# RWKV attention with a Sinkhorn-gated mixture of experts: the first three tiles and the first expert's weights in another order

## The chip, the core and the metric

The kernel runs on one core of a Trainium2 chip. The core's engines work side by side, each through its own list of instructions in order: TensorE (PE in the profile) multiplies matrices, VectorE (DVE), ScalarE (ACT) and GpSimd (POOL) work on elements, and SyncE (SP) mainly issues transfers between memory and the core. They wait for each other by semaphores. The metric is the device time of one execution in microseconds (us). Three executions of the kernel before took 1536.46, 1536.66 and 1537.26 us, so the median is 1536.66.

## What is computed

```python
def _attn_ref(r, k, v, w, u):              # r, k, v: (4, 8, 768, 48)
    state = np.zeros((B, H, D, D)); y = np.zeros_like(r)
    for t in range(S):
        kt, vt, rt = (k[:, :, t], v[:, :, t], r[:, :, t])
        cur = np.einsum('bhd,bhe->bhde', u[None] * kt, vt)
        y[:, :, t] = np.einsum('bhd,bhde->bhe', rt, state + cur)
        state = w[None, :, :, None] * state + np.einsum('bhd,bhe->bhde', kt, vt)
    return y
...
def _moe_ref(x, w_gate, w1, w2):           # N, D, E, F = 3072, 384, 8, 1024
    logits = x @ w_gate
    P = np.exp(logits - logits.max())
    for _ in range(8):
        P /= P.sum(1, keepdims=True) + 1e-09
        P /= P.sum(0, keepdims=True) + 1e-09
        P *= N / E
    for e in range(E):
        out += P[:, e:e + 1] * (np.maximum(x @ w1[e], 0.0) @ w2[e])
    return out
```

The first part is a recurrence over 768 positions for 4 batches of 8 heads with 48 channels each; w is a decay per head and channel. Its output, as a matrix x of 3072 tokens by 384, goes through a gate (eight rounds of normalizing over rows and columns, over all tokens) and through all eight experts, each with two weight matrices w1[e] (384 x 1024) and w2[e] (1024 x 384). Everything is in 32-bit floats.

## The kernel before

**Tiles.** The 3072 tokens are 24 tiles of 128; six tiles are one batch, and a state S is handed from tile to tile in a batch. Three tiles in a row (TH = 3) are a *position*, which the first expert works on together. The recurrence over 128 tokens becomes matrix products: r and k are multiplied by tables of powers of the decay, `rtab` and `ktab` (the powers come from a scan over 64 steps, and 1/w^n is the reciprocal of these powers), and a masked product of the two replaces the loop. Where a decay lies outside 0.7 to 1.1 the tables don't serve; then a flag is set and a branch (`scan_channels`, L386 to L432) works those channels step by step. With the inputs given the branch isn't taken, but each engine has to read the flag (`values_load`, L429) and branch.

**Stages of a tile**, each a function, with the names that its results have in the profile:

- `load_part`: SP loads r, k and v of a tile (`rn`, `kn`, `vn`, 192 KB each; tile 3's r and k go to a part of `hb3`).
- `prep`: POOL makes `rp` = r x `rtab`, DVE makes `kp` = k x `ktab`.
- `bonus_dot` and `bonus`: POOL makes `rk` = r x k x u, DVE sums it over channels to `dg`, and POOL makes v x `dg`.
- `stage_b`: PE transposes `rp` and `kp` (`prT`, `pkT`), ACT copies them out (`rT`, `kT`).
- `stage_c`: PE makes `pA` = kT x rT, DVE copies its upper triangle to `at` under a mask; PE makes `pu`, DVE adds it to the state (`S`).
- `stage_d`: PE makes `py` from the state and `at`; DVE adds the bonus to get `x`, and takes its maximum (`xm`) and from it a power of two as a scale (`xs`).
- `scale_x`: ACT and DVE write x as a high and a low half-precision part (`xsc`).
- `stage_e`: one DMA transposes `xsc` into `hbx` (`DMA_TRANSPOSE` on SP). The expert and the gate read `hbx`.
- `stage_f`: PE multiplies by the gate's weights (`px`), DVE writes the logits (`lparts`).

**The first expert** runs inside this loop as work for PE. `split_weights` (L151) turns its w1 and w2, loaded into `ws0`, into high and low half-precision parts in `ws1`: DVE takes maxima (`wm`, three pieces; `wma`), PE and DVE take them over the partitions (`over_partitions`, `pmax`), then ACT writes high parts and DVE low parts, three pieces of 1024 columns for each matrix. A *unit* is one call of `g1_unit` (nine matmuls `ph` of 384 columns: 128 of the 1024 hidden channels for a whole position; ACT and DVE then write `hb`, high and low) or of `g2_half` (twelve matmuls `po` for half the hidden channels of one tile). `combine_tokens` further prepares sums of tokens, on POOL above all, that the other seven experts need.

**What sets the order.** Every engine's list is written out by hand in program order (`InOrder`, L21): the order of the calls is the order on each engine. The loop at L754 runs i = 0 to 26. In iteration i it issues `prep` and the loads for later tiles, `stage_b` of tile i+1, `scale_x` and `stage_e` of tile i-2, `stage_c` of tile i, `stage_d` of tile i-1, and `stage_f` of tile i-3. So a tile's transposing DMA goes out two iterations after its `stage_c`. At two places `work` puts units into PE's list: one unit, then one or, for i over 8, two. As long as i is 4 or less, `spin(3)` takes the place of a unit: three matmuls of a zero matrix (`pz`), which compute nothing and keep PE busy. The list `side` holds the steps of splitting the weights and of `combine_tokens`; `prepare` takes one step from it, and the table STEPS says how many are taken in iteration i, ahead of and behind `stage_d`. Position 0's units come into the list when tile 2 has gone out. Whatever units are left after the loop are worked one per *tick* (L985), beside the gate's rounds; then the other experts follow, in 14 slots of long runs of matmuls.

**The opening** is all code ahead of the loop: SP's loads (L307 to L328), memsets that clear `hbx`, the flag, the branch, and behind the branch the tables. SP's loads of tile 2's and tile 3's v follow the branch too. PE spins 19 times ahead of the branch, and 5 and 4 times around the tables' transposes.

## Time and profile before

| what | value |
|---|---|
| median of three executions | 1536.66 us |
| the profiled execution, its time | 1537.3 us |
| its span, first to last instruction | 1535.4 us |
| PE busy | 1519.8 us, 99% |
| DVE, ACT, POOL busy | 1033.7, 663.5, 598.1 us (67, 43, 39%) |
| DMA moved | 143.12 MB, 93 GB/s over the span |
| chain of work that ended last | PE 94%, DVE 5% |

The profile is that of one execution. Rows of groups name line, engine, operation, and tiles as out<-in with shape, type and count; almost every row has line 29, the helper that records instructions, so the tile's name tells the place. The timeline has start and duration in us, and in brackets the idle time just ahead with what ended it. PEld is PE's weight load. "DVEq" and "SPq" are the queues of the engines, where branches and issues of DMAs are handled. The stage table gives busy time, with counts in brackets, in stretches of the span; PEclk is PE's granted clock as a share of full speed.

### The profile page before, as it was taken

The page shows a single profiled execution, that of the slowest core. Times are in us where ns is not written, and L with a number is a line of the kernel's source. Part 1 is how long each engine was busy: PE and PEld are TensorE (multiplying, and loading weights), DVE is VectorE, ACT ScalarE, POOL GpSimd, SP SyncE. Part 2 cuts the span into 40 slices and gives each one's busy share as a digit, 9 for nine tenths or more (in the row PEclk, how much of TensorE's full clock was granted, in tenths as well). Part 3 has the DMA queues.
Part 4 walks back from the last instruction along what each step waited for, and adds up shares of the span by engine and source line. Part 5 has one row for each costly group of instructions (what it writes and reads, how often), then busy time and mean ns, then how long its engine had stood idle before and what let it go on. Part 6 is the DMA issues. An engine that isn't in the chain of part 4 may idle for free.

```text
span 1535.4 us, 26169 instructions
## 1 busy us (share of the span) xinstructions
PE 1519.8 (99%) x10313; PEld 858.1 (56%) x10313; DVE 1033.7 (67%) x1714; ACT 663.5 (43%) x1168; POOL 598.1 (39%) x708
## 2 busy tenths in 40 slices
PE   8999999999999999999999999999999999999999
PEld 5677766655555555555555555555555555555555
DVE  8988877676666666667666666656666566666554
ACT  4333424434444444535454444535344444445320
POOL 8789985120213424242424324242423224242200
PEclk9999999999999999999999999999999999999999
DMA  8556623121225665675666666655445554555434
GB/s 192 104 114 113 131 49 112 51 73 55 98 58 109 88 118 86 110 107 83 116 92 125 92 117 88 126 64 98 58 62 92 61 98 56 98 60 98 55 95 129
DMA packets 186847, 143.12 MB, mean 93 GB/s; under 512 B 109537, under 2 KB 180962, under 8 KB 186722
## 3 DMA queue, kind: packets, MB, share of 16 engines
q0 software_dynamic: 44928, 61.36, 32.6%
q1 hardware_dynamic: 141584, 80.07, 19.8%
q8 instruction: 81, 1.33, 0.4%
q14 instruction: 44, 0.36, 0.1%
q10 hardware_dynamic: 210, 0.00, 0.0%
HBM read 55.39 MB, written 80.23 MB: 88 GB/s over the span
## 4 chain that ended last, share of the span: by engine, by line
PE 94%; DVE 5%; issue 0%; ACT 0%; DMA 0%; DVEq 0%; ACTq 0%
PE po L29 48%; PE bZ L29 12%; PE bY L29 12%; PE ph L29 5%; PE bA L29 5%; PE bB L29 5%; PE bC L29 2%; PE py L29 2%; PE pA L29 1%; DVE hb L29 1%; PE prT L29 1%; PE pu L29 1%; DVE at L29 0%; DVE ws L29 0%; PE pkT L29 0%
## 5 line engine op out<-in xcount | busy, mean ns | idle before, releaser
L29 PE MATMUL po<-ws,hbx 128*128 128x384 f16 x3360 | 736.8, 326 | 0.0
L29 POOL DMA_DIRECT2D accd<-stg x288 | 249.7, 869 | 694.4 <-ACT stg L29 673.8
L29 PEld LDWEIGHTS <-hbx 128*128 128x128 f16 x3504 | 334.1, 98 | 292.6
L29 PEld LDWEIGHTS <-ws 128*128 128x128 f16 x3096 | 301.8, 98 | 246.7 <-issue 3.4
L29 ACT ACTIVATE hbx<-tb 128x512 f16<-128x512 f32 x224 | 141.0, 630 | 451.6 <-DVE tb L29 451.6
L29 PE MATMUL po<-ws,hb 128*128 128x384 f16 x1248 | 323.0, 326 | 0.3 <-DVE ws L29 0.3
L29 DVE TENSOR_TENSOR tb<-bY,tb 128x512 f32<-128x512 f32 x168 | 116.1, 691 | 195.4 <-PE bY L29 195.2
L29 ACT ACTIVATE stg<-po,pe 128x384 f32<-128x384 f32 x312 | 179.1, 574 | 121.2 <-PE po L29 94.3
L29 PE MATMUL bZ<-xv,ws 128*128 128x512 f16 x840 | 227.0, 379 | 0.7 <-DVE tb L29 0.7
L29 PE MATMUL bY<-xv,ws 128*128 128x512 f16 x840 | 227.0, 379 | 0.0
L29 DVE TENSOR_TENSOR tb<-bZ,tb 128x512 f32<-128x512 f32 x168 | 115.4, 687 | 136.3 <-PE bZ L29 136.3
L29 PEld LDWEIGHTS <-hb 128*128 128x128 f16 x1248 | 121.4, 98 | 93.8 <-issue 0.8
L29 POOL TENSOR_TENSOR ucb<-rawb 128x256 f32<-128x256 f32 x84 | 75.7, 952 | 118.7 <-DMA rawb<-in_moe_w_dram 118.7
L29 DVE TENSOR_TENSOR tb<-bB,tb 128x512 f32<-128x512 f32 x112 | 77.4, 691 | 48.9 <-PE bB L29 47.0
L29 PE MATMUL ph<-hbx,ws 128*128 128x384 f16 x576 | 105.8, 329 | 1.2 <-DMA hbx<-xsc 0.7
L29 DVE SCALAR_TENSOR_TENSOR hb<-tb,hbx 128x512 f16<-128x512 f32 x112 | 77.2, 689 | 24.7 <-ACT hbx L29 19.5
L29 PE MATMUL bB<-xv,ws 128*128 128x512 f16 x336 | 90.8, 379 | 0.0
L29 PE MATMUL bA<-xv,ws 128*128 128x512 f16 x336 | 90.8, 379 | 0.0
L29 DVE SCALAR_TENSOR_TENSOR hbx<-tb,hbx 128x512 f16<-128x512 f32 x112 | 78.7, 703 | 14.7 <-ACT hbx L29 10.4
L29 ACT COPY tb<-bZ 128x512 f32<-128x512 f32 x56 | 32.8, 585 | 65.5 <-PE bZ L29 65.5
L29 ACT ACTIVATE hb<-ph 128x384 f16<-128x384 f32 x64 | 31.1, 488 | 57.6 <-PE ph L29 57.0
L29 DVE SCALAR_TENSOR_TENSOR hb<-ph,hb 128x384 f16<-128x384 f32 x64 | 35.4, 553 | 26.3 <-ACT hb L29 25.8
(166 smaller groups left out, 1539.6 us busy)
## 6 DMA issues: line engine op xcount, KB each, us to landing
accd<-stg POOLq DMA_DIRECT2D x288, 192.0 KB, 3.7
rawb<-in_moe_w_dram SPq DMA_DIRECT2D x28, 768.0 KB, 6.7
e0d<-stg SPq DMA_DIRECT2D x48, 192.0 KB, 2.1
hb<-e0d SPq DMA_DIRECT2D x48, 192.0 KB, 3.9
vn<-in_v_dram SPq DMA_DIRECT2D x24, 192.0 KB, 3.6
accd<-stg SPq DMA_DIRECT2D x24, 192.0 KB, 1.8
accd<-hb POOLq DMA_DIRECT2D x24, 192.0 KB, 4.7
rawb<-accd SPq DMA_DIRECT2D x24, 192.0 KB, 2.5
```

The source lines that it names most:

```text
L29: return lambda *a, **k: self.tc.keep_in_program_order(f(*a, **k))
```

## The change

It changes the opening and the first iterations of the loop; the stages themselves compute what they did.

- **Tables.** They stand ahead of the branch now. `wsi` holds w and 1/w; one scan of both (520 columns, twice as long) gives the powers of each, and the reciprocal is taken of four columns rather than of 260. The flag comes from the same comparison that the tables need: a maximum per partition, one transpose on PE (`pnb`) and one DVE maximum. A load of w as one row (`wrow`) is gone.
- **Loads.** Ahead of the branch stand r, k of tiles 0 and 1, v of tile 0, u, and w1 in three loads between them. All else follows the branch: v of tile 1, all of tiles 2 and 3, the gate's weights, w2, tile 4.
- **Memsets.** DVE now clears 1920 columns of `hbx` (3072 each for DVE and POOL before), POOL 3840, ACT the rest. Two of the three states are cleared inside the loop.
- **Spins.** 27 matmuls of zeros in all: 8 and 6 ahead of the branch, 4 behind it, and three in each of three places in the loop, where before there were 58 in all.
- **First three tiles.** For i below 3 (AHEAD) an iteration does `stage_d` of its own tile, then `scale_x` and `stage_e` of it (`emit`). From tile 3 on the order is the old one, so iteration 3 has no `stage_d`.
- **Weights.** w1 is split in iteration 0 (its maxima ahead of it), w2 in iterations 1 to 4. STEPS has a third number, for steps behind `emit`; in iterations 5 to 8 no step is taken.
- **First position.** When a tile has gone out, two units of a new kind, `g1_tile`, come into the list: 36 matmuls of 128 columns each (`pht`), half the hidden channels for one tile, and one ACT and one DVE operation of 512 columns behind them. There are six in place of eight `g1_unit`; six `g2_half` of position 0 follow. `work` gives two units to an iteration up to i = 14, and three from 15.

```diff
+    def g1_tile(t, j, W):
...
+        ph = ps1.tile([P, TB], F32, tag="ph", name=f"pht_{t}_{j}")
...
+        for fl in range(FHC):
+            fs = slice((j * FHC + fl) * P, (j * FHC + fl + 1) * P)
+            for c in range(KC):
+                xh_, xl_ = xall(t, 0)[:, c, :], xall(t, 1)[:, c, :]
+                T.matmul(ph[:, fl], w1h[:, c, fs], xh_, start=(c == 0), stop=False)
+                yield
+                T.matmul(ph[:, fl], w1h[:, c, fs], xl_, start=False, stop=False)
+                yield
+                T.matmul(ph[:, fl], w1l[:, c, fs], xh_, start=False, stop=(c == KC - 1))
+                yield
+        S_.activation(hh, ph, AF.Relu)
+        V.scalar_tensor_tensor(hl, ph, 0.0, hh, op0=ALU.max, op1=ALU.subtract)
...
-    for tt in range(2):
-        load_part(tt, "r", r)
-        load_part(tt, "k", k)
...
-    load_part(0, "v", v)
+    def load_w1(c):
+        Q.dma_start(raws[0][:, c], w1[0, c * P : (c + 1) * P, :])
+    load_part(0, "r", r)
+    load_part(0, "k", k)
+    load_w1(0)
     Q.dma_start(
         ub.rearrange("p h d -> p (h d)"),
...
     )
-    load_part(2, "r", r)
-    load_part(2, "k", k)
-    load_part(1, "v", v)
-    load_part(3, "r", r)
-    load_part(3, "k", k)
-    Q.dma_start(wg, w_gate.rearrange("(c p) e -> p c e", p=P))
-    for c in range(KC):
-        Q.dma_start(raws[0][:, c], w1[0, c * P : (c + 1) * P, :])
+    load_part(0, "v", v)
+    load_w1(1)
+    load_part(1, "r", r)
+    load_part(1, "k", k)
+    load_w1(2)
...
-    G.memset(hbx[:, :HB], 0.0)
...
+    Z0, Z1 = 5 * DM, 15 * DM
+    V.memset(hbx[:, :Z0], 0.0)
+    G.memset(hbx[:, Z0:Z1], 0.0)
...
-    fill(hbx[:, 2 * HB :])
-    spin(19)
+    fill(hbx[:, Z1:])
+    spin(8)
...
+    wsi = ac.tile([P, 2, NPAIR], F32, name="wsi")
+    wsafe = wsi[:, 0]
...
+    V.tensor_scalar(wsafe, wt, W_MAX, W_MIN, op0=ALU.min, op1=ALU.max)
+    V.reciprocal(wsi[:, 1], wsafe)
...
+    V.tensor_tensor_scan(
+        pwiv.rearrange("p a n -> p (a n)"), step.rearrange("p a n -> p (a n)"),
+        unit.rearrange("p a n -> p (a n)"), 0.0, op0=ALU.mult, op1=ALU.add,
+    )
...
+    V.tensor_tensor(nb, wt, wsafe, op=ALU.not_equal)
+    V.tensor_reduce(nbm, nb, axis=AX.X, op=ALU.max)
+    V.tensor_tensor(good, wt, wsafe, op=ALU.is_equal)
...
+    spin(6)
+    pnb = ps1.tile([P, TB], F32, tag="ph", name="pnb")
+    T.transpose(pnb[:1, :P], nbm, ident)
+    V.tensor_reduce(flag, pnb[:1, :P], axis=AX.X, op=ALU.max)
...
-    for t_ in ss_:
+    def clear_state(t_):
         for j in range(2):
...
+    clear_state(ss_[0])
...
-    wlim = part(hb3, F32, 2496, (H, D))[:1]
...
-    V.tensor_reduce(flag, wlim, axis=AX.XY, op=ALU.max)
...
+    load_part(1, "v", v)
+    load_part(2, "r", r)
+    load_part(2, "k", k)
     load_part(2, "v", v)
+    load_part(3, "r", r)
+    load_part(3, "k", k)
+    Q.dma_start(wg, w_gate.rearrange("(c p) e -> p c e", p=P))
+    Q.dma_start(raws[1], w2[0].rearrange("(c p) d -> p c d", p=P))
     load_part(3, "v", v)
...
-    V.reciprocal(iv, pw)
...
-    spin(5)
...
-    STEPS = {
-        0: (2, 2), 1: (0, 2), 2: (3, 1), 3: (1, 1),
-        4: (1, 1), 5: (1, 1), 6: (2, 2), 7: (1, 1), 8: (1, 1),
-    }
+    STEPS = {0: (4, 2, 4), 1: (1, 1, 1), 2: (2, 1, 1), 3: (2, 2), 4: (2, 1), 5: (0, 0), 6: (0, 0), 7: (0, 0), 8: (0, 0)}
+    AHEAD = TH
...
+    def emit(tt):
+        scale_x(tt)
+        stage_e(tt)
+        emitted[0] = tt + 1
     prep(0)
+    prepare()
+    stage_b(0)
+    prepare()
     prep(1)
-    stage_b(0)
     bonus_dot(0)
     for i in range(NTT + 3):
         if i == 1:
             gate_max()
-        if i + 2 < NTT:
+        if i == 0:
+            bonus(0)
+            load_chunk(4)
+        elif i + 2 < NTT:
...
-            if i == 0:
-                Q.dma_start(raws[1], w2[0].rearrange("(c p) d -> p c d", p=P))
             prep(i + 2)
         if i + 1 < NTT:
             bonus_dot(i + 1)
         if i + 1 < NTT and i:
             stage_b(i + 1)
-        if 2 <= i <= NTT + 1:
-            scale_x(i - 2)
-            stage_e(i - 2)
-            emitted[0] = i - 1
-        work(1, i > 4)
+        if AHEAD <= i - 2 < NTT:
+            emit(i - 2)
+        work(1, i > 1)
         if i < NTT:
-            bonus(i)
+            if i:
+                bonus(i)
...
             stage_c(i)
+        if i < 2:
+            clear_state(ss_[i + 1])
         if i == 2:
             gate_split(gate_res)
         if i == 0:
             stage_b(1)
         if i <= NTT:
-            work(2 if i > 8 else 1, i > 4)
+            work(2 if i > 14 else 1, i > 0)
         if i == 1:
...
+        if i < AHEAD:
+            stage_d(i)
+        elif AHEAD < i <= NTT:
             stage_d(i - 1)
         for _ in range(n_steps(i)[1]):
             prepare()
+        if i < AHEAD:
+            emit(i)
+            for _ in range(n_steps(i)[2]):
+                prepare()
+            units += [g1_tile(i, j, W) for j in range(2)]
+            if i == AHEAD - 1:
+                units += [g2_half(0, t, j, W) for j in range(2) for t in range(TH)]
+        if i == 0:
+            prep(2)
         if 3 <= i:
             stage_f(i - 3, bank_)
         done = i - 2
-        if 0 <= done < NTT and done % TH == TH - 1:
+        if TH <= done < NTT and done % TH == TH - 1:
             po_ = done // TH
-            if po_ == 0:
-                units += [g1_unit(0, fc, W) for fc in range(FC)]
-                units += [g2_half(0, t, 0, W) for t in range(TH)]
-                pend = [(0, t, 1) for t in range(TH)]
-            for j in range(2 if po_ else 0):
+            for j in range(2):
                 g1 = [g1_unit(po_, fc, W) for fc in range(j * FHC, (j + 1) * FHC)]
                 g2 = [g2_half(*a, W) for a in pend]
                 units += merged(g1, g2)
```

**SP ahead of the branch.** Of its list before, the end (`rn`, `kn`, `vn` are loads of a tile's r, k, v, `ws0` the raw weights, `hb3` tile 3's r and k; the last two rows read the flag and branch):

```order
L29 DMA kn_2_125<-in_k_dram 128x8x48
L29 DMA vn_1_127<-in_v_dram 128x8x48
L29 DMA hb3_73<-in_r_dram 128x8x48
L29 DMA hb3_73<-in_k_dram 128x8x48
L29 DMA wg_119<-in_moe_w_gate_dram 128x3x8
L29 DMA ws0_74<-in_moe_w1_dram 128x1024 x3
L429 TENSOR_LOAD flag_190
L430 COMPARE_AND_BRANCH
```

and of the changed kernel, the whole list behind the load of w:

```order
L29 DMA rn_0_111<-in_r_dram 128x8x48
L29 DMA kn_0_113<-in_k_dram 128x8x48
L29 DMA ws0_74<-in_moe_w1_dram 128x1024
L29 DMA ub_109<-in_u_dram 128x384
L29 DMA vn_0_117<-in_v_dram 128x8x48
L29 DMA ws0_74<-in_moe_w1_dram 128x1024
L29 DMA rn_1_120<-in_r_dram 128x8x48
L29 DMA kn_1_122<-in_k_dram 128x8x48
L29 DMA ws0_74<-in_moe_w1_dram 128x1024
L480 TENSOR_LOAD flag_144
L481 COMPARE_AND_BRANCH
```

Five loads of 192 KB and the gate's weights have left this part of the list, and w1's three loads stand between the tiles' loads instead of behind them.

**SP behind the branch**, in the changed kernel, from tile 3's r and k to the first transposing DMA (four loads of 192 KB, v of tile 1 and r, k, v of tile 2, stand ahead of these rows):

```order
L29 DMA hb3_73<-in_r_dram 128x8x48
L29 DMA hb3_73<-in_k_dram 128x8x48
L29 DMA wg_110<-in_moe_w_gate_dram 128x3x8
L29 DMA ws0_74<-in_moe_w2_dram 128x8x384
L29 DMA vn_3_292<-in_v_dram 128x8x48
L29 DMA rn_4_337<-in_r_dram 128x8x48
L29 DMA kn_4_339<-in_k_dram 128x8x48
L29 DMA vn_4_341<-in_v_dram 128x8x48
L29 DMA_TRANSPOSE hbx_72<-xsc_0_438 128x6x128
```

What left the list ahead of the branch stands here ahead of tile 0's transpose; in the kernel before, v of tiles 2 and 3, r, k, v of tile 4, w2, and r, k, v of tiles 5 and 6 stood there.

**DVE between `dg` of tile 0 and of tile 2.** Before, from the maxima of w1 to tile 0's x:

```order
L29 TENSOR_REDUCE wm_0_319<-ws0_74 128x1 x3
L29 TENSOR_REDUCE wma_0_0_320<-wm_0_319 128x1
L29 TENSOR_REDUCE wgm_315<-wg_119 128x1
L29 TENSOR_TENSOR kp0_168<-hb3_73,ktab_285 128x8x48
L29 TENSOR_REDUCE dg_1_444<-rk_1_350 128x8
L29 COPY_PREDICATED at1_172<-mask_163,pA_1_0_448 128x4x128
L29 COPY_PREDICATED at1_172<-mask_163,pA_1_1_449 128x4x128
L29 TENSOR_TENSOR S1_174<-pu_1_468,S0_173 64x4x48 x2
L29 TENSOR_REDUCE mt_wg_487<-pmax_wg_485 1x1
L29 TENSOR_SCALAR md_wg_489<-ident_84,mt_wg_487 1x1
L29 TENSOR_TENSOR x_0_508<-py_0_491,rk_0_188 128x384
```

and in the changed kernel from tile 0's low part `xsc` to the first `hb`:

```order
L29 SCALAR_TENSOR_TENSOR xsc_0_438<-x_0_426,xs_0_430,xsc_0_438 128x384
L29 SCALAR_TENSOR_TENSOR ws1_75<-ws0_74,sw_0_308,ws1_75 128x1024 x3
L29 TENSOR_TENSOR kp2_175<-kn_2_284,ktab_190 128x8x48
L29 TENSOR_REDUCE wgm_305<-wg_110 128x1
L29 TENSOR_TENSOR kp0_173<-hb3_73,ktab_190 128x8x48
L29 TENSOR_REDUCE dg_1_480<-rk_1_343 128x8
L29 COPY_PREDICATED at1_177<-mask_168,pA_1_0_484 128x4x128
L29 COPY_PREDICATED at1_177<-mask_168,pA_1_1_485 128x4x128
L29 TENSOR_TENSOR S1_179<-pu_1_504,S0_178 64x4x48 x2
L29 SCALAR_TENSOR_TENSOR hb3_73<-pht_0_0_519,hb3_73 128x4x128
```

Tile 0's `xsc` and w1's three low parts stand ahead of `dg` of tile 1 now, and tile 0's first `hb` ahead of tile 1's x; before, x of tile 0 itself came only behind tile 1's S.

**PE in the first two iterations.** Before, from `pu` of tile 1 to the transposes of tile 3 (each matmul of zeros has a row for its weights too):

```order
L29 MATMUL pu_1_468<-vn_1_127,kp1_169 64x48 x8
L29 LDWEIGHTS zeros_108
L29 MATMUL pz_481<-zeros_108 128x512
L29 LDWEIGHTS zeros_108
L29 MATMUL pz_481<-zeros_108 128x512
L29 LDWEIGHTS zeros_108
L29 MATMUL pz_481<-zeros_108 128x512
L29 MATMUL pmax_wg_485<-ident_84,wgm_315 1x128
L29 MATMUL py_0_491<-vn_0_120,at0_171 64x48 x16
L29 MATMUL pmax_w0_0_516<-ident_84,wma_0_0_320 1x128
L29 MATMUL prT_3_533<-ident_84,rp1_167 128x128 x4
L29 MATMUL pkT_3_540<-ident_84,kp0_168 128x128 x4
```

and in the changed kernel from the maximum over partitions of w1 to the first spins of iteration 1,

```order
L29 MATMUL pmax_w0_0_403<-ident_84,wma_0_0_310 1x128
L29 MATMUL py_0_409<-vn_0_117,at0_176 64x48 x16
L29 MATMUL pmax_w0_0_403<-md_w0_0_407,ones_89 128x1
L29 MATMUL prT_2_462<-ident_84,rp0_171 128x128 x4
L29 MATMUL pkT_2_469<-ident_84,kp2_175 128x128 x4
L29 LDWEIGHTS zeros_107
L29 MATMUL pz_476<-zeros_107 128x512
```

and from `pu` of tile 1 to the first matmuls of the first expert:

```order
L29 MATMUL pA_1_1_485<-rT_1_388,kT_1_395 64x128 x2
L29 MATMUL pu_1_504<-vn_1_280,kp1_174 64x48 x8
L29 LDWEIGHTS ws1_75
L29 MATMUL pht_0_0_519<-hbx_72,ws1_75 128x128
L29 LDWEIGHTS ws1_75
L29 MATMUL pht_0_0_519<-hbx_72,ws1_75 128x128
```

Tile 0's `py` comes ahead of tile 2's transposes now, and a unit of the first expert stands where three spins stood.

More of the change, by code (lines that the diff above doesn't have):

```diff
@@ L370, in rwkv_sinkhorn_moe @@
         G.memset(t_[:, :, D:], 0.0)
-    for t_ in ss_:
+    def clear_state(t_):
         for j in range(2):
             G.memset(t_[j * HP : (j + 1) * HP, :, 1 - j, :], 0.0)
+    clear_state(ss_[0])
     fill(at_[0].rearrange("p h c -> p (h c)"))
+    rtab = ac.tile([P, NPAIR, 2, HP], F32, name="rtab")
+    ktab = ac.tile([P, NPAIR, 2, HP], F32, name="ktab")
+    for src, dst in ((tab, rtab), (tabr, ktab)):
+        pt = ps3.tile([P, NPAIR, P], F32, tag="pa", name="pt_tab")
+        for p_ in range(NPAIR):
+            T.transpose(pt[:, p_, :], src[:, p_, :], ident)
+        S_.copy(dst.rearrange("p a j d -> p a (j d)"), pt)
+    fill(at_[1].rearrange("p h c -> p (h c)"))
     rk0 = at2.tile([P, H, D], F32, tag="rk", name="rk_0", bufs=3)
     G.tensor_tensor(rk0, loads[0]["r"], loads[0]["k"], op=ALU.mult)
-    wlim = part(hb3, F32, 2496, (H, D))[:1]
-    flag = ac.tile([1, 1], F32, name="flag")
-    V.tensor_scalar(wlim, wrow, W_MAX, W_MIN, op0=ALU.min, op1=ALU.max)
-    V.tensor_tensor(wlim, wlim, wrow, op=ALU.not_equal)
-    V.tensor_reduce(flag, wlim, axis=AX.XY, op=ALU.max)
     def scan_channels(scratch):
```

55 lines of the change are left out of this document (23 added, 32 removed).

## Prediction

> **What bounds the kernel now.** I read the stage table first (busy time of each engine by stretch; columns: length, then PE, weight loads, DVE, ACT and POOL with their counts, granted clock, DMA share, GB/s).
>
> ```profile
> core 0: us, PE busy (x) PEld busy (x) DVE busy (x) ACT busy (x) POOL busy (x), PEclk, DMA share, GB/s
> 0.00:20.00 20.00, 15.46 (x107) 8.86 (x108) 15.20 (x28) 10.06 (x12) 14.72 (x29) 0.91 0.86 189
> 20.00:40.00 20.00, 16.95 (x273) 11.71 (x271) 18.94 (x42) 7.72 (x13) 18.40 (x20) 0.97 0.89 195
> 40.00:60.00 20.00, 17.60 (x277) 12.72 (x276) 19.53 (x37) 4.71 (x9) 15.20 (x16) 0.86 0.53 104
> 60.00:70.00 10.00, 9.39 (x154) 7.35 (x151) 9.64 (x25) 2.87 (x6) 6.95 (x8) 1.00 0.52 101
> 70.00:100.00 30.00, 29.66 (x453) 21.36 (x451) 28.89 (x56) 12.80 (x23) 21.31 (x21) 1.00 0.51 109
> 100.00:200.00 100.00, 100.00 (x1428) 71.96 (x1426) 83.89 (x167) 39.44 (x73) 94.21 (x102) 1.00 0.62 115
> ```
>
> From 70 us on PE is full, so whatever useful PE work stands done at about 70 us, ahead of or behind before, comes out at the end nearly one for one. Up to there DVE is the full engine (19.53 of 20 from 40 to 60), and PE's busy time is partly empty: the zero matmuls `pz` compute nothing. The group of that tile, and PE in order of time at two places:
>
> ```profile
> L29 PE MATMUL pz<-zeros x58: 379/379/634, 1.3 to 46.8; 128*128 128x512 f16 x58
> ```
>
> ```profile
> 52.76 3.06 PE L29 MATMUL ph<-hbx,ws 128*128 128x384 f16 x9 [0.75 <-DMA hbx<-xsc]
> ...
> 68.97 0.63 PE L29 MATMUL prT<-ident,rp 128*128 128x128 f32 x4
> ...
> 75.70 0.30 PE L29 MATMUL px<-wgp,hbx 128*128 128x16 f16 x6
> 75.87 0.64 PE L29 MATMUL prT<-ident,rp 128*128 128x128 f32 x4
> 76.34 0.60 PE L29 MATMUL pkT<-ident,kp 128*128 128x128 f32 x4
> 76.78 1.63 PE L29 MATMUL ph<-hbx,ws 128*128 128x384 f16 x9
> 78.33 1.10 PE L29 MATMUL pA<-rT,kT 64*64 64x128 f32 x32
> 79.37 0.67 PE L29 MATMUL pu<-vn,kp 128*64 128x48 f32 x16
> 79.97 1.64 PE L29 MATMUL ph<-hbx,ws 128*128 128x384 f16 x9
> 81.54 0.88 PE L29 MATMUL py<-S,rT 128*64 128x96 f32 x16
> 82.25 1.09 PE L29 MATMUL py<-vn,at 128*64 128x48 f32 x32
> ```
>
> From start to start this gives PE's prices: transposes of a tile 0.91 us, pA 1.04, pu 0.60, py 1.8, px 0.17, one unit of expert 0's first layer 1.55. The unit at 52.76, just behind a wait, took 3.06: half speed.
>
> **The change part by part.** DVE sets the opening, so its prices come next (groups of 10 to 100 us), with three moments of its queue, ACT's group, and SP's queue.
>
> ```profile
> L29 DVE COPY_PREDICATED at<-mask,pA 128x512 f32<-128x512 int32 x20 | 13.5, 729 | 0.0
> L29 DVE TENSOR_TENSOR kp<-kn,ktab 128x384 f32<-128x384 f32 x12 | 11.8, 992 | 2.0 <-ACT ktab L29 2.0
> L29 DVE SCALAR_TENSOR_TENSOR ws<-ws,sw,ws 128x1024 f16<-128x1024 f32 x6 | 10.1, 1678 | 0.0
> L29 DVE TENSOR_REDUCE wm<-ws 128x1 f32<-128x1024 f32 x6 | 7.1, 1210 | 0.1
> L29 DVE SCALAR_TENSOR_TENSOR xsc<-x,xs,xsc 128x384 f16<-128x384 f32 x9 | 6.7, 740 | 0.0
> L29 DVE TENSOR_REDUCE dg<-rk 128x8 f32<-128x384 f32 x10 | 5.4, 540 | 0.2 <-DVEq L430 0.2
> L29 DVE TENSOR_REDUCE xm<-x 128x1 f32<-128x384 f32 x9 | 5.0, 553 | 0.3
> L29 DVE TENSOR_TENSOR x<-py,rk 128x384 f32<-128x384 f32 x9 | 4.9, 548 | 0.2
> L29 DVE TENSOR_TENSOR S<-pu,S 64x192 f32<-64x192 f32 x14 | 4.9, 347 | 0.2
> L29 DVE SCALAR_TENSOR_TENSOR hb<-ph,hb 128x384 f16<-128x384 f32 x8 | 4.4, 550 | 0.4 <-ACT hb L29 0.3
> ```
>
> ```profile
> 8.96 1.76 DVE L29 RECIPROCAL hb<-hb 128x260 f32<-128x260 f32 x1
> ...
> 14.03 3.16 DVE L29 TENSOR_TENSOR kp<-kn,ktab 128x384 f32<-128x384 f32 x3 [1.98 <-ACT ktab L29]
> 17.34 0.55 DVE L29 TENSOR_REDUCE dg<-rk 128x8 f32<-128x384 f32 x1 [0.15 <-DVEq L430]
> ```
>
> ```profile
> L29 ACT ACTIVATE ws<-ws,sw 128x1024 f16<-128x1024 f32 x6 | 6.6, 1140 | 1.2 <-DVE sw L29 1.2
> ```
>
> ```profile
> 12.79 1.77 SPq L29 DMA_DIRECT2D ws<-in_moe_w_dram  x3
> 21.02 1.28 SPq L29 DMA_DIRECT2D vn<-in_v_dram  x2
> ...
> 37.62 1.49 SPq L29 DMA_TRANSPOSE hbx<-xsc  x1
> ```
>
> *Tables.* The reciprocal of 260 columns (1.76) becomes one of four columns, the flag's three operations no longer stand ahead of the tables, and a scan twice as long comes in. Tile 0's `dg`, at 17.34 before, I put 3 earlier, at 14.3. Bounds: 0 (POOL's product, now behind the branch, gives it back) and 4 (all of the tables' lead).
>
> *The branch on SP.* SP issues the last w1 piece by 14.56 and nothing until 21.02: 6.5 us at the branch, longer than any issue. The earlier end of its list (six 192 KB loads and three 512 KB pieces instead of eleven and three) brings the next load to about 15: 2.7 MB at the 189 GB/s of the first 20 us take 14. After the branch come ten 192 KB loads and w2 (1.5 MB), 3.5 MB, ahead of tile 0's transposing DMA T0. At 195 GB/s that is 18; before moved the same and one load more between 21.02 and 37.62 (16.6). So T0 lands at 34, between 31 (its bytes at before's pace, nothing added) and 37 (with the longest landing of a transpose):
>
> ```profile
> DMA to landing us min/median/max: 3.0/3.1/4.8
> ```
>
> The w1 pieces pass r1 and k1 on SP. POOL and DVE want those two at about 12.5, when 2.2 MB of the list have moved: just in time, cost 0, at most 1.
>
> *w1 split inside tile 0.* DVE's queue from `dg` of tile 0 to `dg` of tile 1 now holds: dg 0.5, at 1.4, S 0.7, wm 1.2, the maximum over partitions 1.6 (estimate: two turns through PE), x and its scale 1.6, w1's scale 0.5, xsc 0.7, three low parts 3 x 1.68 = 5.0, two kp 2.0, the gate's 0.2: 15.4, so `dg` of tile 1 at 29.7. ACT's three high parts (1.14 each) hide behind the low ones. The kp of tile 2 ends at 28.5, and behind it on PE wait the transposes of tile 2, three spins, pA and pu of tile 1. DVE's masked copy of tile 1 so ends at 32.5 and S at 33.2.
>
> *First position tile by tile.* A unit is now 36 matmuls of 128 columns, 4608 columns; nine of 384 take 1.55, so 2.1 at full speed and 4.1 at the half speed of 52.76. Six of them take 12.4 where eight old units took 12.4: no cost in itself. But `hb` of the unit stands on DVE ahead of tile 1's x, and on PE the unit stands ahead of tile 1's py. So with T0 at 34: unit to 37 (between the two prices), ACT and DVE (about 0.6 each, as for 384 columns 0.55) to 38.0. Then maxima 1.6, x and scale 1.6, a maximum 1.2, xsc 0.7: T1 goes out at 43.4 and lands at 46.5; unit, ACT, DVE to 50.8; py to 51.4 and x to xsc 54.2, T2 lands at 57.4, unit to 59.6. With px of tile 0 (0.2), tile 5's transposes (0.9), unit (2.1), pA, pu (1.6), PE is at 64.4; the first second-layer half waits for w2's second low part, behind that unit on DVE: 59.6, ACT and DVE 1.2, w2's scale 0.5, two low parts 3.4, so 64.7. With the half (2.0), py and px (2.0) PE stands at 68.7, with the overlaps (start to start is 0.05 to 0.1 less than a duration) at 68.5.
>
> *The balance there.* Before, at 68.97 (tile 7's transposes), has one pair of transposes, two pA, one pu, two py and two px more: 0.9 + 2.1 + 0.6 + 3.6 + 0.3 = 7.5. After has eight old units' worth against four, and one second-layer half (2.0): 6.2 + 2.0 = 8.2. So after is 0.7 ahead in work and 0.5 in time: -1.2. The 31 spins fewer are in this already: they filled waits, and waits stay.
>
> *Later.* For i = 9 to 14 an iteration gets two units, not three (the loop as a whole still works off 63 where it was 62). PE then needs 7.6 (the rows from 75.87) and POOL, 94.21 of 100 at three units of some 9.2 us, needs 8.7. Six iterations could lose 1.1 each, 6.6; since POOL's products are used an iteration later, most is covered, so 0 to 6.6, nearer the low end. Iteration 7 has one unit (6.0 on PE against 5.8 on DVE), and iteration 9 three rebuilds on DVE. I take +1.5 for all. The hbx memsets, now shared 1920 to DVE and 3840 to POOL, end before the tables and before the flag: nothing.
>
> Sum against the profiled execution (1537.3, span 1535.4): -1.2 + 1.5 = +0.3. That execution lies 0.6 above the median of 1536.66, so about **1537**.
>
> **The rivals.** *Faster: T0 is there when PE reaches the unit, and the clock stays up.* For it: the landing of 3.0 and the 6.5 us at SP's branch that move forward. Against it: 3.5 MB ahead of T0 in the same queue. It takes 4 from the first wait (the unit at 33 at full speed) and 2 from the second: -1.2 - 6 + 1.5, 1531 to 1532; DVE's 29.7 then bounds the gain, and beyond 9 there is no waste to take before T0.
>
> *Slower: the chain unit, ACT, DVE, py, x, xsc, transpose runs three times in a row with nothing in the other slot.* Before, a tile's transpose had two iterations. For it: 52.76, where a wait of 0.75 was followed by half speed. It decides once PE's wait for T1 is over about 2.5 us: then each round costs the other 2.0 of a half-speed unit, twice, and a landing of 4.8 instead of 3.1 adds 1.7 once: +5.7 and 0.3, 1543. The Trainium skill, "TensorE: Matmul & The Clock Gate" (section "What's actually happening"), says that the clock falls to half after an idle window of about 3.4 us and comes back after as long a busy one; by that only the first unit, behind several us of near idleness, would be slow, and the sum would stay at 1537. The row at 52.76 disagrees in part: its own wait was 0.75.
>
> *Not what it says:* the same work, moved, with nothing saved. That is my forecast's own case.
>
> **How the numbers follow.** This kernel's times tell a change from none at about 0.2%, 3.1 us. No change (1534 to 1540): 0.38. Faster by the early transpose: 0.36; the bounds on T0 (31 to 37) lie on both sides, and DVE sheds w2's maxima and the flag's row from its full stretch. Slower by the chain or POOL: 0.26. The likeliest one's range is 1534 to 1540; over the cases 1528 to 1543, which leaves out a gain over 9 and a loss over 6.
>
> **What would show it.** Right: `dg` of tile 0 near 14.3 and of tile 1 near 30; SP's first load after the branch near 15; PE waiting on the DMA of `hbx` at three places between 30 and 58; PE full from about 69, with the same work done as before. Wrong: the first unit of expert 0 before 32, no half-speed unit (then faster); or `dg` of tile 4 later than 70, or PE idle for POOL or DVE between 100 and 160 (then slower).

## The result, and the profile after

The changed kernel takes 1549.37 us (median of four runs, 1547.75 to 1552.66) where the kernel before takes 1536.74 (four runs, 1536.46 to 1537.26): a ratio of 1.0085, 95% interval 1.0067 to 1.0102. It is slower, by 12.6 us, where no change was forecast, and outside the range of 1528 to 1543. The profiled execution (1547.75) has a span of 1546.0, 10.6 more than before.

The stage table of the changed kernel has the columns of the one shown of before:

```profile
20.00:40.00 20.00, 11.38 (x183) 9.29 (x180) 14.06 (x26) 5.38 (x7) 12.18 (x14) 0.74 0.89 190
40.00:60.00 20.00, 16.35 (x300) 15.19 (x298) 14.81 (x35) 5.57 (x11) 9.64 (x13) 0.91 0.45 81
60.00:70.00 10.00, 9.02 (x162) 7.49 (x162) 8.16 (x15) 5.24 (x8) 5.16 (x7) 1.00 0.21 42
70.00:100.00 30.00, 26.63 (x426) 19.66 (x424) 23.69 (x50) 9.54 (x18) 21.23 (x22) 1.00 0.64 140
100.00:150.00 50.00, 46.68 (x722) 33.94 (x723) 44.12 (x90) 17.86 (x33) 43.54 (x47) 0.97 0.55 103
150.00:200.00 50.00, 49.48 (x729) 35.65 (x719) 41.64 (x81) 18.02 (x33) 48.13 (x52) 1.00 0.56 112
```

From 70 to 200 PE was busy for 26.63 + 46.68 + 49.48 = 122.79 us of 130; before it was 29.66 + 100.00 = 129.66. So 6.9 of the 10.6 are idle time of PE behind the opening. PE's timeline shows where it lies (start, duration, and in brackets the idle time ahead, with what ended it):

```profile
29.90 1.11 PE L29 MATMUL pkT<-ident,kp 128*128 128x128 f32 x4 [7.43 <-DVE kp L29]
...
34.41 2.19 PE L29 MATMUL pht<-hbx,ws 128*128 128x128 f16 x36
...
45.64 3.11 PE L29 MATMUL pht<-hbx,ws 128*128 128x128 f16 x36 [2.24 <-DMA hbx<-xsc]
...
57.28 2.17 PE L29 MATMUL pht<-hbx,ws 128*128 128x128 f16 x36 [1.41 <-DMA hbx<-xsc]
...
69.59 0.64 PE L29 MATMUL prT<-ident,rp 128*128 128x128 f32 x4
...
96.20 1.62 PE L29 MATMUL ph<-hbx,ws 128*128 128x384 f16 x9 [3.37 <-DMA hbx<-xsc]
...
127.45 0.66 PE L29 MATMUL prT<-ident,rp 128*128 128x128 f32 x4 [1.39 <-POOL rp L29]
...
144.71 0.66 PE L29 MATMUL prT<-ident,rp 128*128 128x128 f32 x4 [1.82 <-POOL rp L29]
...
145.64 3.79 PE L29 MATMUL po<-ws,hb 128*128 128x384 f16 x12
...
155.12 0.66 PE L29 MATMUL prT<-ident,rp 128*128 128x128 f32 x4 [0.52 <-POOL rp L29]
```

There are four stops behind 70: 3.37 for the transposed tile 5, and 1.39, 1.82 and 0.52 for POOL's `rp`. Behind the 1.82 a half of the second layer took 3.79, where one at full speed takes 2.12.

To compare two kernels whose PE lists differ I use a *work sum*: up to a given time, each group of matmuls in PE's timeline counts with its full-speed price from start to start (a tile's transposes 0.93, pA 1.04, pu 0.60, py 1.04 or 1.75, px 0.17, a unit 1.56, a `g1_tile` 2.08, a second-layer half 2.06), a group under way counts by the matmuls that have started, and matmuls of zeros count nothing. The difference to the kernel before at the same time says how far ahead (+) or behind (-) a kernel is, in us. It is uncertain by some tenths, as a unit right behind another takes about 0.1 less than these prices. The last column doesn't depend on the prices: it says how much earlier (+) or later (-) than before the first transfer `accd<-stg` on SP starts, which stores the first results of the slots behind the ticks. For all kernels of this study:

```
time                                   70     90    100    120    160    230   accd
changed kernel                       -0.7   -0.1   -3.7   -4.0  -10.6  -10.8  -10.5
e1  transposes ahead of loads        -1.4   -0.8   -2.6   -2.9   -9.3   -9.6   -9.5
e3  three units, four kept back      -0.4   +0.2   -4.9   -4.9   -4.8   -5.1  -10.8
e4  narrow sums on POOL              -1.4   -0.9   -6.0   -6.6   -6.8   -7.0   -6.9
e5  before, two units from 9 to 14    0.0    0.0   -1.3   -5.7   -9.9  -10.0   -9.6
e6  short iterations spread          -2.1   -1.3   -6.0   -6.8   -6.8   -9.7   -9.5
e7  e6, e1, position 1 by tiles      -1.5   -1.0   -1.2   -1.5   -1.5   -2.1   -3.2
e8  e7, two moves in iteration 0     +1.9   +2.6   +2.3   +2.0   +2.0   +1.5   +0.3
e9  the two moves alone              +3.4   +2.6   +0.6   +0.3   -6.2   -6.4   -6.4
e10 e8, one more short iteration     -0.3   +0.4   +0.2   -0.2   -0.1   -0.7    0.0
e11 before, tables early             +0.3   +0.3   +0.3   +0.3   +0.3   +0.3   +0.7
e12 e10, zeros in two waits          +3.4   +3.9   +3.7   +3.4   +3.3   +2.8   +3.5
e13 changed kernel, zeros            +0.3   +0.9   -4.3   -4.7  -11.2  -11.3  -11.1
```

The first row is the result in short: 0.7 behind at the end of the opening, 3.6 lost between 90 and 100, 6.6 lost between 120 and 160, and nothing more behind that. The last column says the same: the first of the 24 transfers `accd<-stg` starts at 357.0 before and 10.5 later in the changed kernel (the rows are those of the tile `accd`, with first and last start):

```profile
L29 SPq DMA_DIRECT2D accd<-stg x24: 319/320/339, 357.0 to 439.1; - x24
```

```profile
L29 SPq DMA_DIRECT2D accd<-stg x24: 319/320/339, 367.5 to 449.6; - x24
```

### The profile page after: what moved, and what is told of

It is laid out like the page before. It is cut to its first block, busy times and chain, and to the rows that moved or that the text cites. A ratio compares the mean times of both kernels' runs of the same rounds, so it can differ in the third digit from the quotient of the medians.

```text
span 1546.0 us, 26389 instructions
## 1 busy us (share of the span) xinstructions
PE 1514.2 (98%) x10427; PEld 860.5 (56%) x10427; DVE 1030.1 (67%) x1712; ACT 663.4 (43%) x1166; POOL 596.6 (39%) x708
## 4 chain that ended last, share of the span: by engine, by line
PE 91%; DVE 4%; POOL 3%; DMA 1%; issue 1%; ACT 1%; POOLq 0%; SPq 0%; DVEq 0%; ACTq 0%
PE po L29 47%; PE bZ L29 12%; PE bY L29 12%; PE bA L29 5%; PE bB L29 5%; PE ph L29 4%; PE bC L29 2%; PE py L29 2%; POOL rk L29 1%; PE pA L29 1%; DMA hbx<-xsc 1%; POOL ws L29 1%; DVE hb L29 0%; DVE ws L29 0%; PE pht L29 0%
## 5 line engine op out<-in xcount | busy, mean ns | idle before, releaser
L29 PEld LDWEIGHTS <-ws 128*128 128x128 f16 x3240 | 307.6, 98 | 247.5 <-issue 5.9
L29 PE MATMUL ph<-hbx,ws 128*128 128x384 f16 x504 | 91.5, 327 | 3.4 <-DMA hbx<-xsc 3.4
L29 DVE TENSOR_REDUCE wms<-rawb 128x1 f32<-128x768 f32 x56 | 51.8, 943 | 0.0
L29 DVE SCALAR_TENSOR_TENSOR ws<-ucb,sw,ws 128x768 f16<-128x768 f32 (+1 forms) x56 | 51.6, 943 | 0.0
```

What stands on the lines that cost most here:

```text
L29: return lambda *a, **k: self.tc.keep_in_program_order(f(*a, **k))
```

## The experiments

Two theories stood at the start. **A**: PE runs out of units near 91, because position 1's units exist only when tile 5 has gone out, and its transposing DMA is late on SP. **B**: with two units in six iterations in a row an iteration of PE is shorter than one of POOL. The rivals put the losses down to the changed opening or to other engines. In the diffs, lines stand as they are in the kernels.

### The number of units, B

*In the kernel before, that edit alone (e5).*

```diff
-            work(2 if i > 8 else 1, i > 4)
+            work(2 if i > 14 else 1, i > 4)
```

> The kernel before, but with two units in place of three in iterations 9 to 14, the change's number, and nothing else of it. Theory B: PE needs 7.6 and POOL about 9, so PE waits for rp there as in the changed kernel: slower by 5 to 8, 1542 to 1545. Rival (the wait belongs to the changed opening): no change, 1537.

1545.82 us, ratio 1.0057 (1.0040 to 1.0074): this one number alone costs the old kernel 9 us, with the old opening. PE's rows in its trace:

```profile
111.45 0.66 PE L29 MATMUL prT<-ident,rp 128*128 128x128 f32 x4 [2.04 <-POOL rp L29]
111.94 0.66 PE L29 MATMUL pkT<-ident,kp 128*128 128x128 f32 x4
112.40 3.78 PE L29 MATMUL po<-ws,hb 128*128 128x384 f16 x12
...
139.02 0.66 PE L29 MATMUL prT<-ident,rp 128*128 128x128 f32 x4 [1.85 <-POOL rp L29]
139.52 0.91 PE L29 MATMUL pkT<-ident,kp 128*128 128x128 f32 x4
140.22 3.03 PE L29 MATMUL ph<-hbx,ws 128*128 128x384 f16 x9
```

Two waits for `rp` make 3.9, and the two units behind them 1.7 and 1.4 more than at full speed: 7.0 of the loss. The changed opening isn't needed for it.

*In the changed kernel, the edit undone (e3).* So that the ticks keep the 35 units they have in the changed kernel (the expectation has 34), fewer are kept back for the first slots.

```diff
-            work(2 if i > 14 else 1, i > 0)
+            work(2 if i > 8 else 1, i > 0)
...
-    e0_last = units[-10:]
-    del units[-10:]
+    e0_last = units[-4:]
+    del units[-4:]
```

> The changed kernel with three units for each iteration from i = 9 again, as in the kernel before; so that the ticks keep 34 units, four units instead of ten are kept back for the first slots. Theory B (POOL): with two units PE needs about 7.6 for an iteration and POOL 8.5 to 9.5, so PE waits for rp (3.7 in all) and loses more to the half clock behind a wait; three units take that away: no wait for rp between 110 and 160, the time falls by 5 to 7, to 1543. Rival (the loss there stems from the late start of POOL's sums at 114.7, not from the number of units): the waits stay, and the time is that of the change, 1549.

1547.66 us, ratio 1.0074 (1.0058 to 1.0091). In the loop B is right: no wait for `rp`, and the work sum stays at -4.9 from 100 to 160 where the changed kernel falls from -3.7 to -10.6. The time hardly shows it: between 230 and the first `accd` the run falls from -5.1 to -10.8, where my second edit acts, as the first slots lack the units kept back.

```profile
300.00:340.00 40.00, 40.00 (x238) 23.58 (x236) 25.71 (x56) 15.05 (x29) 8.10 (x11) 1.00 0.24 82
340.00:380.00 40.00, 36.50 (x187) 18.13 (x186) 32.87 (x59) 17.23 (x31) 0.00 (x0) 1.00 0.12 40
```

PE is idle for 3.5 of the 40 from 340 to 380, waiting for DVE and ACT; before it is busy there throughout. So units aren't free to move: the loop, the ticks and the first slots each need theirs.

*POOL's sums made cheap (e4).* Three quarters of the token sums of the first three groups are left out: 64 columns of 256 are computed.

```diff
+        if sg < 3:
+            b = [x[:, :64] for x in b]
+            v_ = {r_: x[:, :64] for r_, x in v_.items()}
         pool = [
```

> The changed kernel with POOL's sums of tokens for the first three groups made of 64 instead of 256 columns each; three quarters of those sums are left out. Theory B (POOL): one sum falls from 0.75 to some 0.3, an iteration of POOL from about 9 to 7.2, below PE's 7.6, so the waits for rp go and the time falls by 5 to 7, to 1543; the wait of 3.37 at 96 stays. Rival (late units or DVE are what PE waits for there): within 1.5 of 1549.4.

1544.59 us, ratio 1.0047 (1.0030 to 1.0064), 4.8 less than the change. The number of units is the change's, and yet PE waits for nothing between 100 and 160. POOL's group of these sums in that stretch, in the changed kernel and here:

```profile
L29 POOL TENSOR_TENSOR ws<-ws 128x256 f32<-128x256 f32 x17 | 12.8, 767 | 4.1 <-DMA xv<-hbx 3.5
```

```profile
L29 POOL TENSOR_TENSOR ws<-ws 128x64 f32<-128x64 f32 x17 | 7.4, 448 | 4.1 <-DMA xv<-hbx 3.5
```

A quarter of the columns takes 448 ns, not the 300 I had put down, and the four sums of an iteration save 1.3. From 100 to 160 the kernel loses 0.8 of work (-6.0 to -6.8) where the change loses 6.9. It is POOL that PE waits for. That the time fell by 4.8 and not by these 6.1 has its reason ahead of them: the opening ended 0.7 later in this execution, and behind the stop for tile 5 (3.55) a unit took 3.03.

*The same number of units, the short iterations spread (e6).*

```diff
-            work(2 if i > 14 else 1, i > 0)
+            work(2 if i > 8 and i % 3 else 1, i > 0)
```

> The changed kernel with the same number of units in the loop, but the six iterations with two units spread: 9, 12, 15, 18, 21 and 24 instead of 9 to 14. Theory B (POOL is the limit of six short iterations in a row, and has about one iteration of slack): a single short iteration between long ones is covered, no wait for rp, 4 to 6 less than the change, 1544. Rival (POOL's total work is the limit of the loop, wherever the short iterations stand): the same waits at other places, within 1.5 of 1549.

1547.13 us, ratio 1.0066 (1.0048 to 1.0084): 2.2 of the 4 to 6 expected. From 100 to 160 the loss is 0.8 instead of 6.9, with no wait for `rp`, so POOL's total isn't the limit: its slack covers a single short iteration, not six. Part went again elsewhere: at 70 this run was 1.4 behind the change, the stop for tile 5 was 3.38 with a unit of 2.77 behind it (1.62 in the change), and from 160 to 230 2.9 were lost, with two waits of 0.72 and 0.68 for DVE's x.

### The units that run out, A

*The transposing DMA ahead of the loads on SP from iteration 5 on (e1).*

```diff
-            if i + 4 < NTT:
+            if i + 4 < NTT and i < 5:
                 load_chunk(i + 4)
...
             emit(i - 2)
+        if 5 <= i < NTT - 4:
+            load_chunk(i + 4)
```

> The changed kernel, but from iteration 5 on the transposing DMA of a tile stands on SP ahead of the loads of r, k, v instead of behind them. Theory A (SP's queue): the load of v waits until py has let its buffer go, and the transpose of tile 5 stands behind it, issued at 92.16 though xsc was ready at 89.74; PE, out of units, waits for it 3.37 until 96.20. Then here it goes out at about 89.8, PE's wait falls to about 1, and the time falls by 2 to 3, to about 1547. Rival (DVE: xsc itself is what is late, or POOL, the next limit, takes the time back): within 1 of 1549.4.

What stands behind it are these rows of the changed kernel, DVE's and SP's:

```profile
89.14 0.60 DVE L29 SCALAR_TENSOR_TENSOR xsc<-x,xs,xsc 128x384 f16<-128x384 f32 x1
```

```profile
89.37 0.69 SPq L29 DMA_DIRECT2D kn<-in_k_dram  x1
91.70 0.37 SPq L29 DMA_DIRECT2D vn<-in_v_dram  x1
92.16 2.48 SPq L29 DMA_TRANSPOSE hbx<-xsc  x1
```

Tile 5's `xsc` is done at 89.74, and the transpose goes out 2.4 later, behind a load of v that waits until `py` has freed its buffer. With the edit it goes out at 90.45, as `xsc` ends at 90.42 there, and PE's wait falls from 3.37 to 1.55. PE's rows for this wait and for two of those for `rp`:

```profile
95.06 1.64 PE L29 MATMUL ph<-hbx,ws 128*128 128x384 f16 x9 [1.55 <-DMA hbx<-xsc]
...
126.33 0.66 PE L29 MATMUL prT<-ident,rp 128*128 128x128 f32 x4 [1.41 <-POOL rp L29]
...
143.59 0.66 PE L29 MATMUL prT<-ident,rp 128*128 128x128 f32 x4 [2.01 <-POOL rp L29]
```

The opening of this execution ended 0.7 behind the change's, and from 100 on the run is 1.1 to 1.3 ahead of it, at the first `accd` 1.0: the 1.8 stay to the end. The waits for `rp` are about as long as in the change (1.39 and 1.82), only 1.1 earlier, so in the trace POOL doesn't take the gain back, against the rival. The time, 1546.86 (1545.99 to 1550.28), is near the 1547 expected, but by time alone it can't be told from the change's.

*Units while tile 5 is under way (e7)*: e6 and e1 together, and position 1 made of `g1_tile` units, two as soon as each of its tiles is emitted.

```diff
         if AHEAD <= i - 2 < NTT:
             emit(i - 2)
+            if i - 2 < 2 * TH:
+                units += [g1_tile(i - 2, j, W) for j in range(2)]
...
-            for j in range(2):
+            if po_ == 1:
+                units += [g2_half(1, t, 0, W) for t in range(TH)]
+                pend = [(1, t, 1) for t in range(TH)]
+            for j in range(2 if po_ > 1 else 0):
```

> As the run with the six iterations spread, and position 1 worked tile by tile like position 0, so that PE has units while tile 5's transpose is under way, with the transposes ahead of the loads on SP from iteration 5. Theory A (PE ran out of units at 91, the late transpose is only what it then waited for): the wait of 3.4 at 96 is gone altogether, and the time is 3 to 4 below the run with the spread alone, 1541. Rival (POOL or DVE is next there and takes the time back by 130): the same as the spread alone.

1540.28 us, ratio 1.0020 (1.0010 to 1.0030), 6.9 below e6. PE's rows at the place:

```profile
94.86 0.64 PE L29 MATMUL prT<-ident,rp 128*128 128x128 f32 x4
95.33 0.60 PE L29 MATMUL pkT<-ident,kp 128*128 128x128 f32 x4
95.77 2.17 PE L29 MATMUL pht<-hbx,ws 128*128 128x128 f16 x36
```

No stop is left behind 70, and the work sum is nearly flat from 90 on (-1.0, and -2.1 at 230): with the short iterations spread and units at hand, the loop loses little of what the opening leaves. Another 1.1 goes between 230 and the first `accd`, in the ticks (see e10). That it gained 6.9 and not the 3 to 4 of the wait has its reason in the work sum: e6 lost 4.7 between 90 and 100 and 2.9 behind 160, e7 0.2 and 0.6.

### The opening

*Two moves in iteration 0*, in e7 (e8) and in the changed kernel alone (e9).

```diff
-    Q.dma_start(raws[1], w2[0].rearrange("(c p) d -> p c d", p=P))
-    load_part(3, "v", v)
...
             bonus(0)
-            load_chunk(4)
...
             emit(i)
+            if i == 0:
+                Q.dma_start(raws[1], w2[0].rearrange("(c p) d -> p c d", p=P))
+                load_part(3, "v", v)
+                load_chunk(4)
+            if i == 0:
+                prep(2)
             for _ in range(n_steps(i)[2]):
...
-        if i == 0:
-            prep(2)
```

> As the run before, and two more moves in iteration 0: kp of tile 2 on DVE ahead of w1's low parts, and tile 0's transpose on SP ahead of w2, tile 3's v and tile 4's loads. In the changed kernel PE waits 7.43 for kp of tile 2, and the transpose that lands at 34.4 has xsc since 23.57. Theory: w1's last low part, at about 30.5, sets the first unit then, 3 to 4 earlier, and the whole chain of the first three tiles moves with it: 1537 (1535 to 1539). Rival (w2, 1.5 MB later on SP, is late for its maxima on DVE, or x of tile 1 has another limit): within 1.5 of the run before.

> The changed kernel with only the two moves in iteration 0 (kp of tile 2 ahead of w1's low parts; tile 0's transpose ahead of w2, tile 3's v and tile 4's loads). What the opening gains or loses alone: if its time goes to the end, 3 to 4 less than the change, 1545.5. Rival: the later waits for the transpose of tile 5 and for rp take it back, within 1.5 of 1549.

e8: 1535.69 us, ratio 0.9994 (0.9985 to 1.0004); e9: 1545.69, ratio 1.0061 (1.0043 to 1.0079). Both are what was expected, 4.6 below e7 and 3.7 below the change. At 70 the work sum is +1.9 and +3.4, 3.4 and 4.1 more than without the moves. So 3 to 4 us of the changed opening were an order of two queues: kp of tile 2 behind w1's low parts on DVE, and tile 0's transpose behind w2, tile 3's v and tile 4's loads (2.4 MB) on SP. The two moves weren't tried apart. In e9 the later losses are all there (from +2.6 at 90 to -6.2 at 160).

*One more short iteration (e10).* In e8 the lead went from +1.5 at 230 to +0.3 at the first `accd`: counted again, the loop takes 63 units there and leaves 32 for the 33 ticks that the gate's rounds need; with one more short iteration it takes 62 and leaves 33 (the expectation's numbers are one too high).

```diff
-            work(2 if i > 8 and i % 3 else 1, i > 0)
+            work(2 if i > 8 and i % 3 and i != 23 else 1, i > 0)
```

> As the run with the spread, tile by tile for position 1 and the two moves in iteration 0, and one iteration more (23) with two units, so that the loop takes 63 units and 34 are left for the 34 ticks. In that run PE was 2.0 ahead of the kernel before at 230 and 0.1 ahead at 320. If the missing tick is the cause, about 1.5 of it comes back, 1534.2; rival (POOL or DVE has no slack left for one more short iteration): 1535.7 or more.

1535.04 us, ratio 0.9985 (0.9976 to 0.9994), eleven runs from 1533.32 to 1537.36. In its trace the ticks lose nothing more (-0.7 at 230, 0.0 at the first `accd`), but the opening was 2.2 behind e8's, with the same program there: behind a like wait for tile 1's transpose a unit took 4.02, in e8 3.46, and pA of tile 1 1.99 against 1.76. This execution is the slowest of the eleven. The medians of e8 and e10 lie 0.65 apart, which their intervals don't tell from none, so the missing tick is shown by the traces alone. The slow opening led to the next pair.

*Matmuls of zeros in the waits*, in e10 (e12, 8 ahead of tile 2's transposes) and in the changed kernel (e13, 16 there).

```diff
+        if i == 1:
+            spin(8)
         if i + 1 < NTT and i:
             stage_b(i + 1)
...
+        if i == 2:
+            spin(6)
         if i <= NTT:
```

> As the run with 63 units and the two moves in iteration 0, and matmuls of zeros where PE waits in the opening: 8 ahead of tile 2's transposes (wait for kp of 4.2), 6 ahead of the second unit of iteration 2 (wait for the transpose of tile 1 of 2.5, after which the unit took 4.02 for 2.17). Theory (the half clock behind these waits costs some 2 of the opening, and its length makes the spread of the runs): units behind them take 2.2, the time falls by 1.5 to 2.5, to 1533, and the runs lie closer together. Rival (DVE and the transfers set the opening, PE's half speed lies in their shadow): 1535, no change.

> The changed kernel with matmuls of zeros in the same two waits: 16 ahead of tile 2's transposes (wait of 7.43), 6 ahead of the second unit of iteration 2. Theory: the half-speed stretches (pkT 1.11, pA 1.47, pht 3.11, py 1.54 in the changed kernel) go, 1.5 to 2.5 less than the change at 70, and since this comes early it shifts all that follows: 1547. Rival: as above, 1549.

e12: 1532.84 us, ratio 0.9974 (0.9965 to 0.9983), eleven runs from 1531.75 to 1535.86. It beats both kernels, by 4 and by 16.5 us, and e10 by 2.2 in the median (by 3.6 from trace to trace, e10's being its slowest). The unit in question, first in e10 and then in e12; the granted clock over it was 0.50 and 1.00:

```profile
43.95 4.02 PE L29 MATMUL pht<-hbx,ws 128*128 128x128 f16 x36 [2.52 <-DMA hbx<-xsc]
```

```profile
39.91 1.47 PE L29 MATMUL pz<-zeros 128*128 128x512 f16 x6
43.19 2.18 PE L29 MATMUL pht<-hbx,ws 128*128 128x128 f16 x36 [1.81 <-DMA hbx<-xsc]
```

The expected closer spread isn't there (4.1 us against 4.0).

e13: 1548.29 us (1546.50 to 1549.66), not to be told from the change. The unit behind the wait took 2.18 there too, and though kp of tile 2 came at 30.7 instead of 29.9, tile 6's transposes began at 68.65 instead of 69.59, and the work sum at 70 is 1.0 above the change's. The six traces that have the opening of the changed kernel as it is (its own, e1, e3, e4, e6, e7) show these transposes between 69.29 and 70.92, so the zeros seem to gain something in the opening there too, by one trace. What this one gained was lost behind the next stop, where PE's unit took 2.92 and not 1.62 as in the change:

```profile
68.65 0.63 PE L29 MATMUL prT<-ident,rp 128*128 128x128 f32 x4
...
95.21 2.92 PE L29 MATMUL ph<-hbx,ws 128*128 128x384 f16 x9 [3.32 <-DMA hbx<-xsc]
```

At the first `accd` this run is 0.6 behind the change. Whether the zeros gain anything in the time there stays open; in e12, with no stop left behind the opening, they did.

*The tables and the flag ahead of the branch, in the kernel before (e11)*, with the memsets and the spins of the opening that go with them (18 for 28); loads, loop and units are those of before.

```diff
-    spin(19)
+    spin(8)
...
+    V.reciprocal(wsi[:, 1], wsafe)
...
+    spin(6)
+    pnb = ps1.tile([P, TB], F32, tag="ph", name="pnb")
+    T.transpose(pnb[:1, :P], nbm, ident)
+    V.tensor_reduce(flag, pnb[:1, :P], axis=AX.X, op=ALU.max)
...
-    V.reciprocal(iv, pw)
-    spin(5)
```

> The kernel before with one part of the change alone: the tables and the flag ahead of the branch (with their spins, 18 for 28, and the memsets shared as in the change); the loads, the loop and the units are those of before. Theory: dg of tile 0 comes about 2.3 earlier (14.99 in the changed kernel, 17.34 before), DVE is full from 10 to 70, so about 2 comes out at the end: 1534.7. Rival (the transfers, with the same bytes before the branch, set the pace of tiles 1 and 2): 1536.9, no change.

1536.41 us, ratio 0.9996 (0.9987 to 1.0005). DVE's rows for `dg` of tiles 0 and 1:

```profile
14.99 0.55 DVE L29 TENSOR_REDUCE dg<-rk 128x8 f32<-128x384 f32 x1 [0.15 <-DVEq L486]
...
23.89 0.54 DVE L29 TENSOR_REDUCE dg<-rk 128x8 f32<-128x384 f32 x1
```

and that of tile 1 in the kernel before:

```profile
24.22 0.54 DVE L29 TENSOR_REDUCE dg<-rk 128x8 f32<-128x384 f32 x1
```

Tile 0 is 2.35 earlier than before (17.34), tile 1 0.33 (24.22). What comes between them holds the rest, and the work sum is 0.3 ahead throughout: the rival is right that the early tables alone bring next to nothing; that it is the transfers is argued only.

## Why the prediction was wrong

**The opening came nearly when it was forecast, but its balance was counted wrong.** `dg` of tile 0 came at 14.99 (14.3 predicted), of tile 1 at 30.32 (29.7); SP's first load behind the branch at 15.91 (about 15); the first unit started at 34.41 (34), the first of tile 1 at 45.64 (46.5) and of tile 2 at 57.28 (57.4); tile 6's transposes began at 69.59, 1.1 later than the sum's 68.5. Against this the sum held the kernel before at 68.97. The transposes there are the ninth of its trace, those of tile 8 and not of tile 7, so the kernel before had two pairs of transposes more and not one: 0.9 that the sum left out. The balance was put at 1.2 ahead of the kernel before; by the work sum at 70 the changed kernel is 0.7 behind. One unit, the first of tile 1, ran partly at a lower clock (3.11, granted clock 0.67); the first unit, for which the sum took 3, ran at full speed (2.19). The slower rival that I had priced, three rounds of unit, x and transpose, didn't decide: PE's two stops for `hbx` were 2.24 and 1.41, below the 2.5 named there.

**The term "later" was mis-sized.** It gave the six iterations with two units 0 to 6.6 and took +1.5 for all, "since POOL's products are used an iteration later, most is covered". From 120 to 160 they cost 6.6, the upper end. POOL's slack covers a single short iteration (e6); of six in a row PE waits in the fourth (127.45) and the sixth (144.71), and in the iteration behind them, and a wait can add half-speed work behind it, which the bound of 1.1 an iteration didn't have. In e5, where nothing else was changed, they cost 9 us in the time. The condition written down for "slower", PE idle for POOL between 100 and 160, is what the trace shows.

**A step was missed.** Iteration 7 with its single unit was counted (6.0 against 5.8) and put into the same +1.5. What wasn't asked is what PE does next: the twelve units of position 0 are used up, the next one needs tile 5, and tile 5's transpose goes out one iteration before it is wanted, behind a load that waits for PE. The stop was 3.37 and the loss 3.6 (e7 takes it away). In the kernel before the same load stood ahead of each transpose, but older units were always in the list.

**The gain that wasn't there.** The 31 matmuls of zeros that went were replaced by waits, as forecast, and six units done early (14 by iteration 8 instead of 8) are no profit when six are taken out later. The loop works off 62 in both kernels, not 63 in the changed one as the prediction had it, since one call found the list empty. Units taken from iterations 9 to 14 leave POOL uncovered (e5), and units taken from the first slots leave these short (e3).

**The range.** It left out "a loss over 6". The three missed amounts have the same sign: 1537 with 1.9 for the balance (from 1.2 ahead to 0.7 behind), 5.1 for "later" (6.6 for 1.5) and 3.6 for the step missed is 1547.6, with the profiled execution at 1547.75 and the median at 1549.37. The runs of the changed kernel spread by 4.9 us, those of before by 0.8. The profiled run is the fastest of the four, and in it the unit behind the stop for tile 5 ran at full speed (1.62), while behind like stops it took 2.57, 3.03, 2.77 and 2.92 in e3, e4, e6 and e13. That may be about 1 of the 1.6 between the profiled run and the median; it isn't shown, as only one of the four was profiled.

## What to carry to other kernels

Filler work has to be planned for the whole program, not for the place it is moved to: where one engine is full and a second is at 94% of the same stage, taking filler out of several iterations in a row hands the stage to the second engine. When a change makes a list of work shorter, look for the moment at which the list is empty, and follow what its next entry waits for, with all that stands ahead of it in that queue. Losses of separate stages add up, and so do their cures: e9's 3.7 and e7's 9.1 below the change each left a kernel slower than before, together they made 13.7 (e8), and with the ticks and the clock mended one that is faster (e12). Where a gain doesn't show in the time, the next place has to be looked at before the move is given up: e3 lost its gain in the first slots, e13 behind the next stop.

## What the runs showed of the hardware

How long a stop is doesn't by itself decide whether PE's clock falls. Half-speed work stood behind stops of 1.82 (3.79 for 2.12, granted clock 0.55), 1.85 (3.03 for 1.62, granted clock 0.52), 2.04 (3.78) and, in part, 2.24 (3.11 for 2.17). At one and the same place, the stop for tile 5, the unit took 1.62, full speed, behind 3.37 in the changed kernel, and 2.57, 3.03, 2.77 and 2.92 behind 3.19, 3.55, 3.38 and 3.32 in e3, e4, e6 and e13. The Trainium skill, "TensorE: Matmul & The Clock Gate" (section "What's actually happening"), says that activity is watched in a window of about 3.4 us that runs freely and isn't reset when a kernel starts, and that the clock falls after at least one idle window. A free-running window agrees with the scatter in these rows; that a whole idle window is needed doesn't agree with the stops of 1.8 to 2.2. No run here shows the window itself.

A sum on POOL took 767 ns for 256 columns and 448 for 64: if the rest grows in proportion to the width, about 340 ns don't depend on it, an estimate from these two rows.
